# Identity products as fillers in TensorE's waits at the seam between forward and backward

## The chip, the cores and the metric

One core of a Trainium2 chip. The metric is the device time of one execution in microseconds. The kernel before has a median of 1434.71 us over three runs.

## What is computed

A decode step of an adaptively modulated transformer block and its gradients, in bfloat16: one query token, 32 heads of 192 with a cache of 8192 keys and values each, then a small MLP. The kernel returns the block's output and the gradients of nine inputs, the whole K and V caches among them.

```python
mod = (silu(c) @ w_mod).reshape(6, ...)            # sa, ca, ga, sb, cb, gb
h  = layernorm(x) * (1 + ca) + sa
q  = (h @ wq)                                      # 32 heads x 192
p  = softmax(q @ k_cache.T * 192 ** -0.5)          # 8192 positions a head
x  = x + ga * ((p @ v_cache) @ wo)
h  = layernorm(x) * (1 + cb) + sb
x  = x + gb * (h + gelu(layernorm(h) @ w3) @ w4)   # the mixing part has one position: it adds nothing
# returned: x and the gradients of x, k_cache, v_cache, wq, wo, w3, w4, c, w_mod
```

With one query, dV of a head is the outer product of its softmax weights and the gradient of its output, dK that of its score gradients and the query. The score gradients need V times the output gradient over all positions.

## The kernel before

**Forward.** A loop over heads streams K and V in halves of 4096 positions (tiles KB and VB, 128 partitions x 32 positions x 192). It ends with the MLP and its backward.

**The seam.** After the last head come the MLP's matmuls, the layer-norm gradients lb2 and lb1, `do_mm` (output gradient of a pair of heads, broadcast over partitions, tile do_r) and `c_ps` (one correction per head). Nearly all of it is one chain of small operations. `layernorm_bwd` builds lb_pr on VectorE, gets two means from a TensorE matmul into PSUM (`mean_mm`, tile mean_ps), calls `fill()` if it has one, and then reads the means (lb_s, line 128). In lb2 the fill transposes the second half of a block of wo (`do_t(TL, 8)`).

**Backward.** 64 steps (32 heads x 2 halves, from the last head down). A step s

- reduces dP out of PSUM (line 314) and forms dS on VectorE,
- makes dV in eight groups (`dv_groups`): four TensorE matmuls of one row each into a two-bank PSUM tile (line 877; two such tiles exist), then one ScalarE evacuation (line 878),
- multiplies V of the next step with do_r on VectorE in two halves (`mul_q`, line 857) and sums each product on TensorE with 12 matmuls of 128x256 against the identity (`tree_q`, line 866, here called a tree),
- makes dK in two halves on VectorE (`dk_part`, line 882),
- stores dV and dK through POOL's queue, and loads V of step s+4 through SP's (line 295).

Output tiles rotate through five buffers, V through three. A prologue ahead of step 0 makes the first half of dV and the products for step 0. Steps 0 and 1 (the last head) also get their query gradient from the K tile (`dq_rows`: dq_ps, then two pairs of matmuls into columns 0 and 1 of dq_c at lines 1109 and 1110, read on VectorE at lines 1111 and 1112).

**Side work.** Four times in a step, `slot()` runs the next piece of a list: w4 and w3 gradients, transposes of wo (wT_ps, line 746), broadcasts (bc_t, bc_ps), later the gradients of wq and w_mod.

**Order.** The program order is the order of each engine; it is written out by hand (`manual_schedule` over TensorE, VectorE, ScalarE and SyncE). Waits between engines come from the tiles' uses. All small PSUM results share one buffer, tag "s" of pool psS, one bank.

Of the kernel before, what the change touches and what calls it, by code (L numbers as in the profile page):

```python
# [8 lines left out]
FP32 = mybir.dt.float32  # L9
# [11 lines left out]
def kernel(  # L21
# [27 lines left out]
    P = 128  # L49
    D = A_x.shape[-1]  # L50
    _, HQ, S, DH = A_k_cache.shape
# [9 lines left out]
    ND = D // P  # L61
# [56 lines left out]
        return tmp.tile([P, n], dtype, name=name)  # L118


    def mean_mm(src, n):
        ps = psS.tile([P, 16], FP32, name="mean_ps", tag="s")
        T_.matmul(ps[:, 0:n], lhsT=onesD, rhs=src, start=True, stop=True)
        return ps

# [38 lines left out]
    def layernorm_bwd(dn, n, r, add, out, name, fill=None):  # L164
        pr = tcol(2 * ND, "lb_pr")
        V_.tensor_copy(out=pr[:, 0:ND], in_=dn)
        V_.tensor_tensor(out=pr[:, ND : 2 * ND], in0=dn, in1=n, op=ALU.mult)
        s = mean_cols(pr, 2, "lb_s", fill)
        t1 = tcol(ND, "lb_t1")
        V_.tensor_scalar(out=t1, in0=n, scalar1=s[:, 1:2], scalar2=s[:, 0:1], op0=ALU.mult, op1=ALU.add)  # L170
        t2 = tcol(ND, "lb_t2")
        V_.tensor_tensor(out=t2, in0=dn, in1=t1, op=ALU.subtract)
        V_.scalar_tensor_tensor(out=out, in0=t2, scalar=r[:, 0:1], in1=add, op0=ALU.mult, op1=ALU.add)

    def bcast_cols(src, n, out, eng):
        tp = psS.tile([NF, P], FP32, name="bc_t", tag="s")
        T_.transpose(out=tp[0:n, :], in_=src, identity=ident_f)
        rows = tmp.tile([NF, P], BF16, name="bc_rows")
        eng(out=rows[0:n, :], in_=tp[0:n, :])
        for g in range(0, n, 4):  # L180
            m = min(4, n - g)
            ps = psB.tile([P, 512], FP32, name="bc_ps", tag="b")
            for b in range(m):
                T_.matmul(ps[:, b * P : (b + 1) * P], lhsT=pick(n, g + b), rhs=rows[0:n, :], start=True, stop=True)
            eng(out=out[:, g * P : (g + m) * P], in_=ps[:, 0 : m * P])

    def store_vec(src, dram, name):
        tp = psS.tile([NF, P], FP32, name="sv_t", tag="s")
        T_.transpose(out=tp[0:ND, :], in_=src, identity=ident_f)
        rows = tmp.tile([ND, P], BF16, name="sv_rows")  # L190
        V_.tensor_copy(out=rows, in_=tp[0:ND, :])
        nc.gpsimd.dma_start(out=dram.rearrange("o (i p) -> (o i) p", p=P), in_=rows)
# [581 lines left out]
    n2_bf = tcol(ND, "n2_bf", BF16)  # L774
    V_.tensor_copy(out=n2_bf, in_=n2)
    w3t(2)()
    ups = psS.tile([P, NF], FP32, name="u_ps", tag="s")
    for a in range(NF):
        for k in range(ND):
            T_.matmul(ups[:, a : a + 1], lhsT=w3v[k][:, a * P : (a + 1) * P], rhs=n2_bf[:, k : k + 1], start=(k == 0), stop=(k == ND - 1))  # L780
# [30 lines left out]
                T_.matmul(h2_ps[:, k : k + 1], lhsT=w4r(a)[:, k * P : (k + 1) * P], rhs=g_bf[:, a : a + 1], start=(a == 0), stop=(a == NF - 1))  # L811

    h2_mm(0, 2)
    dn_ps = psS.tile([P, ND], FP32, name="dn_ps", tag="s")
    for k in range(ND):
        for a in range(NF):
            T_.matmul(dn_ps[:, k : k + 1], lhsT=w3Tv[a][:, k * P : (k + 1) * P], rhs=du_bf[:, a : a + 1], start=(a == 0), stop=(a == NF - 1))
# [12 lines left out]
    V_.tensor_copy(out=d_n2, in_=dn_ps)  # L830
    h2_mm(2, ND)
    do_t(TL, 0)
    layernorm_bwd(d_n2, n2, r2, dbo, d_sb, "lb2", lambda: do_t(TL, 8))
    d_n1 = tcol(ND, "d_n1")
    V_.scalar_tensor_tensor(out=d_n1, in0=cb, scalar=1.0, in1=d_sb, op0=ALU.add, op1=ALU.mult)
    dw4_rows(flat(KX), 0, 3)
    dw4_store(flat(KX), 0, 3)
    V_.tensor_tensor(out=bo, in0=h2_ps[:, 0:ND], in1=h_b, op=ALU.add)
    layernorm_bwd(d_n1, n1, r1, dy_c, dx1, "lb1")
    V_.tensor_tensor(out=dao_bf, in0=dx1, in1=ga, op=ALU.mult)  # L840
    do_mm(TL)
    V_.tensor_tensor(out=dao, in0=dx1, in1=ga, op=ALU.mult)
    V_.tensor_tensor(out=ao, in0=aoP, in1=aoN, op=ALU.add)

    c_ps = psS.tile([P, HQ], FP32, name="c_ps", tag="s")
    for k in range(ND):
        T_.matmul(c_ps, lhsT=dao[:, k : k + 1].to_broadcast([P, P]), rhs=AO[:, k, :], start=(k == 0), stop=(k == ND - 1))
    V_.tensor_tensor(out=cpr, in0=c_ps, in1=rinv, op=ALU.mult)
# [16 lines left out]
        for k in range(0, DH, TS):  # L865
            T_.matmul(ps[:, q * JQ : (q + 1) * JQ, :], lhsT=ident_bf, rhs=pq[:, q, :, k : k + TS], start=(k == 0), stop=(k == DH - TS), skip_group_check=True)  # L866

    def dv_groups(dV, er, doh, gs):

        dV4 = dV.rearrange("p (r k) d -> p r (k d)", r=4)  # L870
        for g in gs:
            m, q = divmod(g, 2)
            ps = psV.tile([P, 2, 512], FP32, name="dv_ps", tag="v")
            for k in range(2):
                for b in range(2):
                    p0 = 32 * (2 * q + b)
                    T_.matmul(ps[:, b, k * DH : (k + 1) * DH], lhsT=er[p0 : p0 + 1, 2 * m + k, :], rhs=doh[p0 : p0 + 1, :], start=True, stop=True)  # L877
            A_.copy(out=dV4[:, 2 * q : 2 * q + 2, m * PW : (m + 1) * PW], in_=ps[:, :, 0:PW])  # L878

    def dk_part(dK, qh, dS4, lo, hi):  # L880
        n = hi - lo
# [25 lines left out]
            cur["next"] = w  # L907

    def g_bcast(src, n, out):
        tp = psS.tile([NF, P], FP32, name="bc_t", tag="s")  # L910
        T_.transpose(out=tp[0:n, :], in_=src, identity=ident_f)
        rows = tmp.tile([NF, P], BF16, name="bc_rows")
        V_.tensor_copy(out=rows[0:n, :], in_=tp[0:n, :])
        yield
        for g in range(0, n, 4):
            m = min(4, n - g)
            ps = psB.tile([P, 512], FP32, name="bc_ps", tag="b")
            for b in range(m):
                T_.matmul(ps[:, b * P : (b + 1) * P], lhsT=pick(n, g + b), rhs=rows[0:n, :], start=True, stop=True)
            A_.copy(out=out[:, g * P : (g + m) * P], in_=ps[:, 0 : m * P])  # L920
            yield
# [15 lines left out]
    def g_chunk(b, first, v3, rows, dst, n, acc, lay):  # L937

        lo = n * CW
        if first:  # L940
            cur["w"] = cur.pop("next")
        w = stg = cur["w"][:, :, b * PW : (b + 1) * PW]
        cols = lambda a, b_: [(l, r, w[:, a, c0 : c0 + r - l]) for bb, l, r, c0 in lay if bb == b_]
        v_bf = tcol(3, "v_bf", BF16)
        V_.tensor_copy(out=v_bf, in_=v3)
        yield
        wT = bst.tile([P, 15 * P], BF16, name="wT", tag="wT")
        transposed(0, cols, ND, wT)
        tp = psS.tile([NF, P], FP32, name="bc_t", tag="s")
        T_.transpose(out=tp[0:3, :], in_=v3, identity=ident_f)  # L950
        vrow = tmp.tile([3, P], BF16, name="vrow")
        V_.tensor_copy(out=vrow, in_=tp[0:3, :])
        yield
        transposed(8, cols, ND, wT)
        bp = psB.tile([P, 512], FP32, name="bc_ps", tag="b")
        for bb, l, r, c0 in lay:
            T_.matmul(bp[:, c0 : c0 + r - l], lhsT=pick(3, bb), rhs=vrow[:, l:r], start=True, stop=True)
        v_bc = bst.tile([P, PW], BF16, name="v_bc")
        A_.copy(out=v_bc, in_=bp[:, 0:PW])  # L959
        yield  # L960
        ps = psS.tile([P, ND], FP32, name="acc_ps", tag="s")
        for i in range(ND):
            for bb in range(3):
                T_.matmul(ps[:, i : i + 1], lhsT=wT[:, (bb * ND + i) * P : (bb * ND + i + 1) * P], rhs=v_bf[:, bb : bb + 1], start=(bb == 0), stop=(bb == 2))
        for i in range(3):
            V_.tensor_scalar(out=stg[:, i, :], in0=v_bc, scalar1=rows[:, i : i + 1], scalar2=None, op0=ALU.mult)
        yield
        V_.tensor_tensor(out=acc, in0=ps, in1=acc, op=ALU.add)
        for i in range(3, ND):
            V_.tensor_scalar(out=stg[:, i, :], in0=v_bc, scalar1=rows[:, i : i + 1], scalar2=None, op0=ALU.mult)  # L970
        if first:
            next_w()
        else:
            nc.gpsimd.dma_start(out=dst[:, :, lo : lo + CW], in_=cur["w"])
        yield
# [124 lines left out]
    def dq_rows(t, kb, dS4):  # L1100

        ps = psB.tile([P, 512], FP32, name="dq_ps", tag="b")
        for j in range(JH):
            p0 = 32 * (j % 4)
            T_.matmul(ps[p0 : p0 + 32, 0:DH], lhsT=dS4[:, j, 0:1].to_broadcast([P, 32]), rhs=kb[:, j, :], start=(j < 4), stop=(j >= JH - 4), skip_group_check=True)
        row = bst.tile([P, DH], FP32, name="dq_junk")
        A_.copy(out=row, in_=ps[:, 0:DH])
        cp = psS.tile([P, 4], FP32, name="dq_c", tag="s")
        T_.matmul(cp[:, 0:1], lhsT=row[:, 0:P], rhs=c32[:, 0:1], start=True, stop=True)
        T_.matmul(cp[64:128, 1:2], lhsT=row[:, P:DH], rhs=c32[:, 0:1], start=True, stop=True)  # L1110
        V_.tensor_tensor(out=dq_x[:, 2:3], in0=cp[:, 0:1], in1=dq_x[:, 2:3], op=ALU.add)
        V_.tensor_tensor(out=dq_x[64:128, 1:2], in0=cp[64:128, 1:2], in1=dq_x[64:128, 1:2], op=ALU.add)
# [5 lines left out]
    dV0 = OB[0]  # L1118
    er = er_l.pop(0)
    ps = psR.tile([P, JH, TS], FP32, name="dot_ps")  # L1120
    dv_groups(dV0, er, do_of(H1), (0, 2))
    mul_q(0, 0)
    tree_q(ps, 0)
    dv_groups(dV0, er, do_of(H1), (4, 6))
    dv_store(0, dV0, 0, JQ)
    mul_q(0, 1)
    tree_q(ps, 1)
    for s in range(NS):
        h, t = ht(s)
        nxt = s + 1 < NS  # L1130
        doh = do_of(h)
        qh = qs_bc[:, h * DH : (h + 1) * DH]
        assert not nxt or (s + 1) // 4 in done
        dP = tcol(JH, "dP")
# [10 lines left out]
        slot()  # L1145
        dV, dK = OB[(2 * s) % len(OB)], OB[(2 * s + 1) % len(OB)]
        if s == 0:
            dv_groups(dV, er, doh, (1, 3))
        else:
            er = er_l.pop(s)  # L1150
            dv_groups(dV, er, doh, (0, 1, 2, 3))
        if nxt:
            ps = psR.tile([P, JH, TS], FP32, name="dot_ps")
            mul_q(s + 1, 0)
# [1 line left out]
        slot()  # L1156
        dk_part(dK, qh, dS4, 0, JQ)
        if s > 0:
            dv_groups(dV, er, doh, (4, 5))
        slot()  # L1160
        dv_groups(dV, er, doh, (5, 7) if s == 0 else (6, 7))
        if s + 2 < NS:
            er_l[s + 2] = load_er(s + 2)
        dv_store(s, dV, JQ if s == 0 else 0, JH)
# [45 lines left out]
```

## Time and profile before

| what | value |
|---|---|
| runs | 1433.92, 1434.71, 1446.62 us |
| profiled execution, its own time | 1435.39 us |
| its span, first to last instruction | 1433.6 us |
| mean granted TensorE clock | 0.766 |
| busy, PE / DVE / ACT | 78% / 77% / 61% |
| moved by DMA | 569.37 MB, 397 GB/s over the span |
| TensorE matmuls | 12739 |

The span is cut into 40 slices of 35.8 us. The clock rows give what was granted in tenths of full speed. A row of the table of stretches gives the length, the busy time of each engine with its instructions in brackets, the granted clock, the DMA engines' busy share and GB/s. In the timeline and the chain, a row starts with its start and its length in us; brackets at the end give the engine's idle time before it and what ended that.

### The profile page before, as it was taken

Reading aid. Unit: us, or ns where it says so; the run is one execution under the profiler, and the core shown is the slowest. Engines: PE = TensorE matmul, PEld = TensorE weight load, DVE = VectorE, ACT = ScalarE, POOL = GpSimd, SP = SyncE. Lnnn points to the kernel's source line nnn. Section 1 sums busy time; section 2 is a strip of 40 time slices with the busy share of each in tenths; the row PEclk is TensorE's granted clock in tenths of the full one; section 3 lists DMA queues with packets and bytes.
Section 4 is the critical chain, followed back from the end, with each engine's and each line's share of the span. In section 5 each row is a group of like instructions: output and inputs, shape, how many; then the busy total and the mean of one; then the engine's idle time right before and its main releaser. Section 6 shows DMA issues by size and latency. Waiting matters only on the chain.

```text
span 1433.6 us, 30378 instructions
## 1 busy us (share of the span) xinstructions
PE 1112.0 (78%) x12739; PEld 788.9 (55%) x12739; DVE 1100.2 (77%) x1397; ACT 880.0 (61%) x1965; POOL 144.9 (10%) x255
## 2 busy tenths in 40 slices
PE   3988989999999998775687776777767577777764
PEld 2777777777877777543444443444434344444432
DVE  4989899999999987456677676667767667676764
ACT  0777777777877776554665565556655556555644
POOL 0000000000000000111111111111111111111111
PEclk9999999999999998565656566566666766656565
DMA  9999999999999994489999999999999999999997
GB/s 375 397 418 418 411 417 415 414 416 413 418 415 411 420 411 180 156 308 407 423 406 425 423 417 423 409 419 417 418 426 427 403 425 418 422 414 416 416 406 315
DMA packets 77432, 569.37 MB, mean 397 GB/s; under 512 B 8782, under 2 KB 26526, under 8 KB 36974
## 3 DMA queue, kind: packets, MB, share of 16 engines
q1 hardware_dynamic: 50842, 340.44, 58.8%
q0 software_dynamic: 26432, 226.97, 37.7%
q8 instruction: 100, 1.64, 0.5%
q14 instruction: 38, 0.31, 0.1%
q10 hardware_dynamic: 20, 0.00, 0.0%
HBM read 340.95 MB, written 226.43 MB: 396 GB/s over the span
## 4 chain that ended last, share of the span: by engine, by line
PE 24%; DMA 11%; DVE 10%; issue 8%; ACT 7%; POOL 1%; POOLq 0%; ACTq 0%; SPq 0%; DVEq 0%
PE dot_ps L866 15%; DVE pq L857 5%; ACT KB L878 5%; DMA out_dram<-KB 4%; DMA er_b<-eT_d 4%; PE wT_ps L746 3%; PE dv_ps L877 3%; DMA VB<-in_A_v_cache_dram 2%; ACT wT L747 1%; DVE KB L882 1%; DMA wo_st<-in_A_wo_dram 1%; DVE dP L314 1%; PE do_ps L759 1%; DVE dq_junk L986 1%; ACT v_bc L959 0%
## 5 line engine op out<-in xcount | busy, mean ns | idle before, releaser
L878 ACT CAST KB<-dv_ps 128x768 bf16<-128x768 f32 x512 | 375.9, 815 | 170.5 <-PE dv_ps L877 170.2
L866 PE MATMUL dot_ps<-pq,ident_bf 128*128 128x256 bf16 x1536 | 325.7, 395 | 51.0 <-DVE pq L857 50.7
L357 ACT ACTIVATE vs<-VB,Ef 128x192 bf16<-128x192 bf16 x872 | 315.0, 447 | 0.0
L877 PE MATMUL dv_ps<-do_r,er_b 1*128 1x192 bf16 x2048 | 174.3, 311 | 147.2 <-ACT KB L878 132.6
L866 PEld LDWEIGHTS <-ident_bf 128*128 128x128 bf16 x1536 | 201.9, 135 | 152.0 <-issue 79.1
L882 DVE TENSOR_TENSOR KB<-qs_bc,dS 128x3072 bf16<-128x3072 bf16 x128 | 223.9, 1750 | 26.0 <-DMA out_dram<-KB 19.6
L300 DVE TENSOR_TENSOR prod<-KB,qs_bc 128x6144 bf16<-128x6144 bf16 x62 | 207.8, 3352 | 29.1 <-DMA KB<-in_A_k_cache_dram 17.5
L857 DVE TENSOR_TENSOR pq<-VB,do_r 128x3072 bf16<-128x3072 bf16 x126 | 220.3, 1749 | 2.7 <-DMA VB<-in_A_v_cache_dram 2.7
L877 PEld LDWEIGHTS <-er_b 1*128 1x128 bf16 x2048 | 64.8, 102 | 243.9 <-issue 225.7
L372 PE MATMUL mp<-vs,KB 128*128 128x193 bf16 x1984 | 189.8, 248 | 4.0 <-ACT vs L357 2.9
L372 PEld LDWEIGHTS <-KB 128*128 128x128 bf16 x1984 | 169.9, 98 | 13.2 <-DMA KB<-in_A_k_cache_dram 5.9
L747 ACT COPY wT<-wT_ps 128x1024 bf16<-128x1024 bf16 x84 | 81.0, 964 | 156.6 <-PE wT_ps L746 156.6
L310 PE MATMUL half_ps<-prod,ident_bf 128*128 128x256 bf16 x744 | 95.1, 279 | 46.0 <-DVE prod L304 45.7
L350 DVE TENSOR_TENSOR vs<-VB,E 128x1728 bf16<-128x1728 bf16 (+1 forms) x122 | 127.1, 1062 | 0.3 <-ACT vs L357 0.3
L314 DVE TENSOR_REDUCE dP<-dot_ps 128x32 f32<-128x512 f32 x64 | 44.1, 688 | 97.8 <-PE dot_ps L866 97.7
L304 DVE TENSOR_TENSOR prod<-prod 128x3072 bf16<-128x3072 bf16 x62 | 108.7, 1753 | 1.0
L310 PEld LDWEIGHTS <-ident_bf 128*128 128x128 bf16 x744 | 72.9, 99 | 64.2 <-issue 55.2
L377 PE MATMUL mp<-vs,KB 128*64 128x193 bf16 x1984 | 106.5, 250 | 0.0
L377 PEld LDWEIGHTS <-KB 128*64 128x64 bf16 x1984 | 79.6, 110 | 19.6 <-issue 19.6
L337 ACT ACTIVATE E<-S_h,negm 128x256 bf16<-128x256 f32 x31 | 15.8, 508 | 115.6 <-DVE negm L498 113.3
L704 POOL DMA_DIRECT2D er_b<-eT_d x64 | 36.9, 577 | 488.4 <-PE dv_ps L877 474.5
L432 POOL DMA_DIRECT2D eT_d<-er x16 | 8.8, 548 | 555.2 <-ACT vs L348 517.7
(269 smaller groups left out, 1008.0 us busy)
## 6 DMA issues: line engine op xcount, KB each, us to landing
out_dram<-KB POOLq DMA_DIRECT2D x127, 1536.0 KB, 17.1
VB<-in_A_v_cache_dram SPq DMA_DIRECT2D x123, 1536.0 KB, 12.0
KB<-in_A_k_cache_dram SPq DMA_DIRECT2D x64, 1536.0 KB, 11.3
wo_st<-in_A_wo_dram SPq DMA_DIRECT2D x31, 480.0 KB, 11.8
w_st<-in_A_wq_dram SPq DMA_DIRECT2D x12, 960.0 KB, 12.9
out_dram<-wo_st POOLq DMA_DIRECT2D x16, 480.0 KB, 18.9
out_dram<-stg POOLq DMA_DIRECT2D x7, 960.0 KB, 18.7
out_dram<-w_st POOLq DMA_DIRECT2D x7, 960.0 KB, 21.8
```

The lines of the kernel that those rows point to most:

```text
L300: V_.tensor_tensor(out=prod, in0=src, in1=vec[:, None, :].to_broadcast([P, JH, DH]), op=ALU.mult)
L304: V_.tensor_tensor(out=prod[:, :, 0:HW], in0=prod[:, :, 0:HW], in1=prod[:, :, DH - HW : DH], op=ALU.add)
L310: T_.matmul(ps, lhsT=ident_bf, rhs=prod[:, :, k : k + TF], start=(k == 0), stop=(k == w - TF))
L350: V_.tensor_tensor(out=vs[:, 0:n, 0:DH].rearrange("p j (a b) -> p j a b", b=4), in0=v[:, v0 : v0 + n, :].rearrange("p j (a b) -> p j a b", ...
L357: A_.activation(out=vs[:, k, 0:DH], in_=v[:, v0 + k, :], func=ACT.Copy, scale=Ef[:, j0 + k : j0 + k + 1])
L372: T_.matmul(mp[:, 0:MW], lhsT=kb[:, j0 + k, 0:P], rhs=vs[:, k, 0:MW], start=(q == 0 and k == 0), stop=(z and k == JQ - 1), skip_group_chec ...
L377: T_.matmul(mp[p0 : p0 + 64, MO : MO + MW], lhsT=kb[:, j0 + k, P:DH], rhs=vs[:, k, 0:MW], start=False, stop=(z and k >= JQ - 2), skip_grou ...
L857: V_.tensor_tensor(out=pq[:, q], in0=v_l[s][:, q * JQ : (q + 1) * JQ, :], in1=do_of(ht(s)[0])[:, None, :].to_broadcast([P, JQ, DH]), op=AL ...
L866: T_.matmul(ps[:, q * JQ : (q + 1) * JQ, :], lhsT=ident_bf, rhs=pq[:, q, :, k : k + TS], start=(k == 0), stop=(k == DH - TS), skip_group_c ...
L877: T_.matmul(ps[:, b, k * DH : (k + 1) * DH], lhsT=er[p0 : p0 + 1, 2 * m + k, :], rhs=doh[p0 : p0 + 1, :], start=True, stop=True)
L878: A_.copy(out=dV4[:, 2 * q : 2 * q + 2, m * PW : (m + 1) * PW], in_=ps[:, :, 0:PW])
L882: V_.tensor_tensor(out=dK[:, lo:hi, :].rearrange("p j (a b) -> p j a b", b=4), in0=qh.rearrange("p (a b) -> p a b", b=4)[:, None, :, :].to ...
```

## The change

Every tile of tag "s" that is made in these parts now comes from `s_tile`, as the front of a whole bank of 512 columns, and `s_bank` remembers the latest. `keep(n)` issues n matmuls of 128x256, the identity against a part of qs_bc, into columns 256 to 511 of that latest bank. Nothing reads these columns. `keep` is called in the two layer-norm gradients, in the prologue, and behind each dV group of steps 0 to 5. The five other tiles that now come from `s_tile` (bc_t twice, sv_t, u_ps, acc_ps) are changed in the same one-line manner.

```diff
+    s_bank = {}
+    def s_tile(n, name, rows=P):
+        s_bank["t"] = psS.tile([P, 512], FP32, name=name, tag="s")
+        return s_bank["t"][0:rows, 0:n]
+    def keep(n):
+        for _ in range(n):
+            T_.matmul(s_bank["t"][:, 256:512], lhsT=ident_bf, rhs=qs_bc[:, 0:256], start=True, stop=True, skip_group_check=True)
+
     def mean_mm(src, n):
-        ps = psS.tile([P, 16], FP32, name="mean_ps", tag="s")
+        ps = s_tile(16, "mean_ps")
...
-    dn_ps = psS.tile([P, ND], FP32, name="dn_ps", tag="s")
+    dn_ps = s_tile(ND, "dn_ps")
...
-    layernorm_bwd(d_n2, n2, r2, dbo, d_sb, "lb2", lambda: do_t(TL, 8))
+    layernorm_bwd(d_n2, n2, r2, dbo, d_sb, "lb2", lambda: (do_t(TL, 8), keep(4)))
...
-    layernorm_bwd(d_n1, n1, r1, dy_c, dx1, "lb1")
+    layernorm_bwd(d_n1, n1, r1, dy_c, dx1, "lb1", lambda: keep(6))
...
-    c_ps = psS.tile([P, HQ], FP32, name="c_ps", tag="s")
+    c_ps = s_tile(HQ, "c_ps")
...
-    def dv_groups(dV, er, doh, gs):
+    def dv_groups(dV, er, doh, gs, busy=0):
...
             A_.copy(out=dV4[:, 2 * q : 2 * q + 2, m * PW : (m + 1) * PW], in_=ps[:, :, 0:PW])
+            keep(busy)
...
-        cp = psS.tile([P, 4], FP32, name="dq_c", tag="s")
+        cp = s_tile(4, "dq_c")
...
-    dv_groups(dV0, er, do_of(H1), (0, 2))
+    dv_groups(dV0, er, do_of(H1), (0, 2), 3)
...
-    dv_groups(dV0, er, do_of(H1), (4, 6))
+    dv_groups(dV0, er, do_of(H1), (4, 6), 1)
...
+        busy = 2 if s < 6 else 0
...
-            dv_groups(dV, er, doh, (1, 3))
+            dv_groups(dV, er, doh, (1, 3), busy)
...
-            dv_groups(dV, er, doh, (0, 1, 2, 3))
+            dv_groups(dV, er, doh, (0, 1, 2, 3), busy)
...
-            dv_groups(dV, er, doh, (4, 5))
+            dv_groups(dV, er, doh, (4, 5), busy)
...
-        dv_groups(dV, er, doh, (5, 7) if s == 0 else (6, 7))
+        dv_groups(dV, er, doh, (5, 7) if s == 0 else (6, 7), busy)
```

More of the change, by code (lines that the diff above doesn't have):

```diff
@@ L175, in bcast_cols @@
     def bcast_cols(src, n, out, eng):
-        tp = psS.tile([NF, P], FP32, name="bc_t", tag="s")
+        tp = s_tile(P, "bc_t", NF)
         T_.transpose(out=tp[0:n, :], in_=src, identity=ident_f)
@@ L187, in store_vec @@
     def store_vec(src, dram, name):
-        tp = psS.tile([NF, P], FP32, name="sv_t", tag="s")
+        tp = s_tile(P, "sv_t", NF)
         T_.transpose(out=tp[0:ND, :], in_=src, identity=ident_f)
@@ L776 @@
     w3t(2)()
-    ups = psS.tile([P, NF], FP32, name="u_ps", tag="s")
+    ups = s_tile(NF, "u_ps")
     for a in range(NF):
@@ L909, in g_bcast @@
     def g_bcast(src, n, out):
-        tp = psS.tile([NF, P], FP32, name="bc_t", tag="s")
+        tp = s_tile(P, "bc_t", NF)
         T_.transpose(out=tp[0:n, :], in_=src, identity=ident_f)
@@ L948, in g_chunk @@
         transposed(0, cols, ND, wT)
-        tp = psS.tile([NF, P], FP32, name="bc_t", tag="s")
+        tp = s_tile(P, "bc_t", NF)
         T_.transpose(out=tp[0:3, :], in_=v3, identity=ident_f)
@@ L960, in g_chunk @@
         yield
-        ps = psS.tile([P, ND], FP32, name="acc_ps", tag="s")
+        ps = s_tile(ND, "acc_ps")
         for i in range(ND):
```

## The prediction

> **What bounds the kernel now.** I read the granted clock of the core first (mean 0.766), then the 40 slices of the page.
>
> ```profile
> PEclk9999999999999998565656566566666766656565
> DMA  9999999999999994489999999999999999999997
> ```
>
> In the forward pass TensorE has its full clock, in the backward about six tenths of it. The DMA engines are busy nearly everywhere but in slices 16 to 18. The table of stretches says it more sharply (length, then busy us of PE, PEld, DVE, ACT and POOL, granted clock, DMA share, GB/s):
>
> ```profile
> 585.00:640.00 55.00, 40.37 (x313) 24.59 (x312) 33.13 (x33) 31.55 (x47) 7.77 (x13) 0.56 0.68 245
> 640.00:1380.00 740.00, 534.33 (x4442) 321.91 (x4440) 523.84 (x764) 419.31 (x589) 119.96 (x205) 0.63 1.01 418
> ```
>
> From 640 us on the kernel is bound by bytes: 418 GB/s, the rate that the forward has too. A faster TensorE buys nothing there. Only the seam between the passes can give time back. From 585 to 640 us 245 GB/s move instead of 418, which is 55 x (1 - 245/418) = 22.8 us of missing transfers. Until about 592 us there is hardly anything to move: the first dV store is issued at 591.77 us. So some 7 us of this can't be filled and about 15 us is the most that faster steps can win. That is hardly more than 1% of the time (14.3 us), which is about what a measurement of this kernel can tell from no change.
>
> In the chain of work that ended last, restricted to 584 to 640 us, the trees of line 866 hold 35.5%, more than anything else. One of them here, and one late in the backward at the full clock (timeline):
>
> ```profile
> 586.73 2.72 PE dot_ps L866 x12
> 688.60 1.48 PE L866 MATMUL dot_ps<-pq,ident_bf 128*128 128x256 bf16 x12
> ```
>
> So the clock is worth 1.24 us a tree. A single slow one of these matmuls takes 0.421 us and a fast one 0.269; the spacing is therefore (2.72 - 0.42)/11 = 0.21 us slow and (1.48 - 0.27)/11 = 0.11 us fast. A filler has the same form, 128x256 against the identity, and costs the same.
>
> **When the clock rises.** The clock changes in steps of 3.41 us, so I cut the seam into stretches of that length, along its changes:
>
> ```profile
> 584.30:587.72 3.42, 1.85 (x14) 1.23 (x14) 3.08 (x6) 1.50 (x2) 0.00 (x0) 0.50 0.20 72
> 587.72:591.13 3.41, 3.41 (x22) 2.05 (x20) 0.62 (x1) 1.16 (x2) 0.00 (x0) 0.50 0.00 0
> ...
> 597.96:601.37 3.41, 3.41 (x22) 2.06 (x21) 1.03 (x1) 2.76 (x4) 1.83 (x3) 0.50 0.45 98
> ...
> 611.61:615.02 3.41, 3.41 (x21) 1.69 (x19) 0.00 (x0) 0.19 (x1) 0.00 (x0) 0.50 0.42 177
> 615.02:618.44 3.42, 2.07 (x27) 1.39 (x20) 1.94 (x2) 3.33 (x6) 0.58 (x1) 1.00 0.10 18
> ...
> 632.09:635.50 3.41, 3.15 (x18) 2.11 (x17) 2.27 (x3) 0.97 (x2) 1.65 (x3) 0.50 0.69 202
> 635.50:638.92 3.42, 1.18 (x23) 0.67 (x20) 3.38 (x4) 2.74 (x5) 0.00 (x0) 1.00 1.02 304
> ```
>
> A stretch is granted the full clock for what the one before it did. Busy time is not the measure: 587.72 and 597.96 are filled without a gap, and the clock stays at half. They hold almost one tree each, cut at an edge, and dV matmuls of a single row. The stretch from 611.61 has 8 tree matmuls and five do_ps of 384 columns, together 15.5 fillers' worth; that from 632.09 has a whole tree and four broadcasts. So some 12 full matmuls of 256 columns (3072 columns) in one stretch are the threshold, and several stretches lie just under it.
>
> The Trainium skill, "TensorE: Matmul & The Clock Gate", section "What's actually happening", puts the window at 3413 ns and grants the full clock after one busy window. The length agrees with the 3.41 us here; if any busy matmul counted, 587.72 would already have raised the clock, and it didn't.
>
> **The change, part by part.** By the diff I count 4 + 6 fillers in the two layer-norm gradients, 3 x 2 + 1 x 2 in the prologue, 2 x 4 in step 0 and 2 x 8 in each of steps 1 to 5: 106, a little below the 110 of its title. No transfer is added or moved; bank "s" keeps its one buffer.
>
> *Layer-norm gradients.* The fillers go into the bank that holds the means, between the mean matmul and its reader lb_s. Does the reader wait for them, though it reads other columns? The dq_c tile answers:
>
> ```profile
> 603.70 0.59 PE L1109 MATMUL dq_c<-c,dq_junk 128*128 128x1 f32 x2 [0.43 <-ACT dq_junk L1107]
> 604.22 0.37 PE L1110 MATMUL dq_c<-c,dq_junk 128*64 128x1 f32 x2
> 604.63 0.16 DVE L1111 TENSOR_TENSOR dq_x<-dq_c,dq_x 128x1 f32<-128x1 f32 x1 [5.64 <-PE dq_c L1110]
> ```
>
> Line 1111 reads column 0, which line 1109 wrote, and still it starts only behind line 1110, which writes column 1. So I take it that a reader waits for every earlier write into its tile. The Trainium skill, "PSUM — Partial Sum Buffer", section "PSUM bank collisions raise a hardware error", asks for the same: guard by bank, not by address. This speaks against an "unread part" being free; by addresses alone this term would be 0.85 us.
>
> The stage before the change:
>
> ```profile
> 577.25 0.17 DVE L128 TENSOR_REDUCE lb_s<-mean_ps 128x2 f32<-128x10 f32 x1 [1.74 <-PE mean_ps L123]
> 577.98 0.91 PE L746 MATMUL wT_ps<-ident_bf,wo_st 128*128 128x128 bf16 x7 [0.76 <-ACT wT L747]
> 578.82 0.57 PE L123 MATMUL mean_ps<-lb_pr,onesD 128*128 128x10 f32 x2
> 579.43 0.17 DVE L128 TENSOR_REDUCE lb_s<-mean_ps 128x2 f32<-128x10 f32 x1 [0.76 <-PE mean_ps L123]
> 580.65 0.82 PE L759 MATMUL do_ps<-wT,dao_bf 128*128 128x384 bf16 x2 [1.25 <-DVE dao_bf L840]
> ```
>
> The first lb_s now waits for the transposes (end 578.89) and 4 x 0.21: 579.75 instead of 577.25, 2.5 us later. From there to the second mean matmul it is 1.42 us of VectorE (lb_pr ends at 578.67), then 0.58, then 6 x 0.21 = 1.28: the second lb_s starts at 583.05 instead of 579.43. do_ps starts 3.65 us later. The clock is half here, and the 7 x 128 + 4 x 256 = 1920 columns ahead of it don't raise it. Taken: **+3.65**, since the dq_x row is the nearest; lower bound +0.85, where only TensorE's order delays the second mean.
>
> *Fillers in the prologue and the steps.* The six behind groups 0 and 2 take 1.28 us and lie in TensorE's wait of 1.57 us for the first pq product; without that cover they would cost their 1.28. In a step, a group's matmuls wait for ScalarE's evacuation (0.60 us each: 132.6 us over 220 waits), which covers 2 fillers at 0.42. Uncovered are those of the last group before a tree: 0.42 us at half clock in the prologue, 0.84 a step. Only steps 0 to 2 come ahead of saturation: 0.42 + 3 x 0.84 = 2.9 slow, 1.5 fast. Taken: **+2.2**. Bounds: nothing, if all are covered, and 106 x 0.21 = 22.3 us together with the layer norms, if none is.
>
> *The clock.* On the chain seven trees between 586 and 636 us run slow: 7 x 1.24 = 8.7 us. Its other TensorE pieces there (dV groups, dq, transposes, do_ps) sum to 8.8 us; of these I give 3.5 to the clock, less than half, as latency doesn't shrink. Always fast would be worth 12.2 us. How much of it comes? Of the 14 half-clock stretches from 584.30 to 635.50, the tree matmuls number 5, 14, 9, 11, 14, 3, 0, 6, 8, 5, 0, 9, 5 and 12. Sixteen fillers over a step of 11 to 17 us are about 4 a stretch. With these, 7 of 14 pass twelve (counting do_ps). So I take half: **-6.1**, between 0 and 12.2.
>
> Sum: 3.65 + 2.2 - 6.1 = -0.25 us. The profiled execution has a span of 1433.6 and a time of 1435.39; the runs have a median of 1434.71. On the median that gives **1434.5 us**.
>
> **Rivals.**
> *The clock holds.* Once fast, a step is shorter, its columns are denser, and no stretch falls below the threshold until step 6. For it: several stretches lie just under twelve. Against: TensorE still waits for ScalarE (2.9 us for four evacuations), where two fillers per 0.7 us are only 10 a stretch. Time: 3.65 + 1.5 - 12.2 = -7 us, 1427.7; with the reader not waiting, 1424.9. This is also what the skill's rule of any busy window would make of it.
> *The fillers only queue: slower.* The clock stays at half from do_ps on; TensorE, in order, does its fillers ahead of the next tree, and the first stores come later. It decides from the point where clearly fewer than half of the stretches rise, for at half the sum is nought; with none it is 3.65 + 2.9 = +6.5 us, **1441.2**; with the covers gone too, up to 1457. For it: the fillers' first ten lie in a stage with few columns. Against: 587.72 needs two or three more.
> *The lead is lost in the transfers.* From 618 us the DMA share is 0.9 or more, so only the five trees before it count: half of 5 x 1.24 = 3.1 is won, 3.65 + 2.2 paid, +2.8 us, 1437.5. Against: holes of 0.44 to 0.69 up to 635 us.
>
> **How the numbers follow.** Forecast 0.45, clock holds 0.25, fillers queue 0.2, lost in transfers 0.1. The range runs from 1424 (clock holds, no wait for lb_s) to 1446 (queueing, with two thirds of the further covers kept). Faster by over 1% would need the whole 15 us of fillable transfers, 0.12; slower by over 1% would need some two thirds of all fillers uncovered, 0.14; the rest, 0.74, is within 1%.
>
> **What would show it.** Right: the second lb_s some 3.6 us later, beginning behind a filler; full clock in about half of the stretches from 588 to 640 us; the dP reduce of step 4 (now at 648.73) within 4 us of that; 418 GB/s unchanged behind it. Wrong: an lb_s ahead of the fillers; a clock that stays full from 588 us on, or at half; DMA saturated more than 5 us earlier or later than 640.

## The result, and the profile after

The changed kernel has a median of 1442.24 us over 20 runs (1435.31 to 1447.59), the kernel before, on the same chip, 1435.93 us over 20 (1431.05 to 1446.62). The ratio is 1.0042 with a 95% interval of 1.0027 to 1.0057: about 6.0 us slower. That is inside the range and, as forecast, within 1%, but the forecast was no change, and the kernel became slower by more than its interval.

The page of the profile after shows the clock and the DMA engines' share in 40 slices of 36.0 us:

```profile
span 1440.0 us, 30591 instructions
PEclk7899999999999998667556566556665666656656
DMA  9999999999999994389999999999999999999998
```

The low stretch of the DMA row lies in the same slices as before and is a little deeper (4, 3, 8 instead of 4, 4, 8). The table of stretches for the same two windows as before (length, busy us of PE, PEld, DVE, ACT and POOL, clock, DMA share, GB/s):

```profile
585.00:640.00 55.00, 47.41 (x358) 25.98 (x359) 30.49 (x41) 29.28 (x43) 7.78 (x13) 0.69 0.62 227
640.00:1380.00 740.00, 544.00 (x4476) 325.98 (x4475) 522.26 (x763) 419.94 (x590) 118.20 (x202) 0.64 1.01 415
```

So the clock did rise in the seam, from 0.56 to 0.69, and yet fewer bytes move there: 227 GB/s instead of 245.

The layer-norm gradients in the timeline after:

```profile
578.42 0.55 PE L135 MATMUL mean_ps<-lb_pr,onesD 128*128 128x10 f32 x2
580.42 1.06 PE L131 MATMUL mean_ps<-qs_bc,ident_bf 128*128 128x256 bf16 x4
581.52 0.17 DVE L140 TENSOR_REDUCE lb_s<-mean_ps 128x2 f32<-128x10 f32 x1 [4.26 <-PE mean_ps L131]
583.52 1.44 PE L131 MATMUL mean_ps<-qs_bc,ident_bf 128*128 128x256 bf16 x6
585.00 0.17 DVE L140 TENSOR_REDUCE lb_s<-mean_ps 128x2 f32<-128x10 f32 x1 [2.05 <-PE mean_ps L131]
586.21 1.78 PE L771 MATMUL do_ps<-wT,dao_bf 128*128 128x384 bf16 x5 [1.26 <-DVE dao_bf L852]
```

Line 131 is the filler in `keep`, line 140 the read of the means. The first mean is complete at 578.97, but lb_s starts at 581.52, 0.04 us behind the last filler, and its idle time is put down to line 131. The second lb_s does the same.

The forward of this execution came 1.75 us later, so times below are counted from the copy of d_n out of PSUM ahead of the first layer-norm gradient (575.08 us before, 576.83 us after). A second profile of the changed kernel (the last experiment) agrees with the first to 0.3 us in every column.

| from the d_n copy, us | do_ps | dP step 0 | step 2 | step 4 | step 5 | step 6 | full clock up to 72 us, start (length) |
|---|---|---|---|---|---|---|---|
| before | 5.57 | 17.8 | 49.1 | 73.7 | 86.3 | 103.5 | 39.9 (3.4), 60.4 (3.4), 67.3 (3.4) |
| after | 9.39 | 22.3 | 50.3 | 77.5 | 90.9 | 109.5 | 22.8 (10.2), 39.9 (10.2), 70.6 (3.4) |

By these two profiles the changed kernel is 4.5 us late at step 0, wins 3.3 of it back in steps 0 and 1, where it has full clock for part of the time, and loses 2.6 again in steps 2 and 3 at half clock. At step 6 it is 6.0 us late. The loss in steps 2 and 3 comes again in the second profile (27.3 us for the two, 24.6 before); whether the 3.3 us are owed to the fillers is taken up at e9_late_only.

### The profile page after: what moved, and what is told of

Its sections match the earlier page's. It is cut to its first block, busy times and chain, and to the rows that moved or that the text cites. A ratio compares the mean times of both kernels' runs of the same rounds, so it can differ in the third digit from the quotient of the medians.

```text
span 1440.0 us, 30591 instructions
## 1 busy us (share of the span) xinstructions
PE 1133.2 (79%) x12845; PEld 796.4 (55%) x12845; DVE 1101.1 (76%) x1397; ACT 881.1 (61%) x1965; POOL 144.8 (10%) x255
## 4 chain that ended last, share of the span: by engine, by line
PE 26%; DVE 10%; issue 8%; ACT 8%; DMA 7%; POOL 1%; POOLq 0%; ACTq 0%; DVEq 0%
PE dot_ps L878 16%; DVE pq L869 5%; ACT KB L890 5%; PE wT_ps L758 3%; PE dv_ps L889 3%; DMA er_b<-eT_d 3%; DMA VB<-in_A_v_cache_dram 2%; DMA out_dram<-KB 1%; ACT wT L759 1%; DVE KB L895 1%; DVE dP L326 1%; PE do_ps L771 1%; DMA out_dram<-stg 1%; DVE dq_junk L999 1%; ACT v_bc L972 1%
## 5 line engine op out<-in xcount | busy, mean ns | idle before, releaser
L878 PE MATMUL dot_ps<-pq,ident_bf 128*128 128x256 bf16 x1536 | 322.0, 392 | 50.5 <-DVE pq L869 50.1
## 6 DMA issues: line engine op xcount, KB each, us to landing
VB<-in_A_v_cache_dram SPq DMA_DIRECT2D x123, 1536.0 KB, 11.6
```

## The experiments

Ratios are against the kernel before on the same chip, with 95% intervals; a thousandth is 1.4 us. Diffs are against the changed kernel. The relative times are from one profile each. LN fillers are the ten in the layer-norm gradients, group fillers the 96 in the prologue and behind the dV groups of the steps.

| kernel | LN fillers | group fillers | ratio | us | dP step 0 | dP step 4 | clock 585 to 640 us |
|---|---|---|---|---|---|---|---|
| before | none | none | 1 | 0 | 17.8 | 73.7 | 0.56 |
| after | means' bank | 96 | 1.0042 [1.0027, 1.0057] | +6.0 | 22.3 | 77.5 | 0.69 |
| e1_ln_only | means' bank | none | 1.0029 [1.0013, 1.0045] | +4.2 | 21.6 | 77.6 | 0.56 |
| e2_no_ln | none | 96 | 1.0012 [0.9991, 1.0033] | +1.7 | 18.5 | 73.9 | 0.69 |
| e3_ln_other_bank | free bank | 96 | 0.9989 [0.9971, 1.0007] | -1.6 | 18.2 | 72.9 | 0.73 |
| e4_one_row | means' bank, one row | 96, one row | 1.0044 [1.0026, 1.0063] | +6.3 | 22.3 | 79.6 | 0.59 |
| e5_two_steps | free bank | prologue, steps 0, 1 | 0.9974 [0.9956, 0.9992] | -3.7 | 14.3 | 67.2 | 0.81 |
| e6_before_tree | free bank | the same, 4 ahead of a tree in steps 2 to 5 | 0.9957 [0.9939, 0.9974] | -6.2 | 18.2 | 71.9 | 0.71 |
| e7_one_each | free bank | 1 a group in the steps | 0.9983 [0.9967, 0.9999] | -2.4 | 17.6 | 72.5 | 0.72 |
| e8_four_each | free bank | 4 a group in the steps | 0.9984 [0.9970, 0.9997] | -2.3 | 14.3 | 68.1 | 0.88 |
| e9_late_only | none | steps 2 to 5 | 0.9999 [0.9982, 1.0015] | -0.1 | 17.1 | 70.7 | 0.69 |
| e10_denser_ln | free bank, closer | prologue, steps 0, 1 | 0.9967 [0.9947, 0.9986] | -4.7 | 13.8 | 67.0 | 0.81 |
| e11_ln_other_only | free bank | none | 0.9977 [0.9963, 0.9991] | -3.3 | 16.7 | 71.4 | 0.60 |

**Only the LN fillers (e1_ln_only).**

```diff
-    dv_groups(dV0, er, do_of(H1), (0, 2), 3)
+    dv_groups(dV0, er, do_of(H1), (0, 2))
...
-    dv_groups(dV0, er, do_of(H1), (4, 6), 1)
+    dv_groups(dV0, er, do_of(H1), (4, 6))
...
-        busy = 2 if s < 6 else 0
+        busy = 0
```

> Only the 4 + 6 fillers of the layer-norm gradients are kept. Theory (the means' readers wait for the fillers, and the seam's delay goes straight into the end): do_ps starts 9.4 us after the copy of d_n, as in the changed kernel, instead of 5.6; the clock afterwards as before the change; time +3 to +4 us (ratio 1.002 to 1.003). Rival (the later DMA-bound part takes the delay up): do_ps as late, time within 1 us of before.

Measured: +4.2 us, between 1.9 and 6.5. do_ps comes 9.38 us behind the d_n copy as in the whole change, and step 4 is 3.9 us late. The ten fillers alone cost about what do_ps is late.

**Only the group fillers (e2_no_ln).** The two layer-norm gradients are called as before.

```diff
-    layernorm_bwd(d_n2, n2, r2, dbo, d_sb, "lb2", lambda: (do_t(TL, 8), keep(4)))
+    layernorm_bwd(d_n2, n2, r2, dbo, d_sb, "lb2", lambda: do_t(TL, 8))
...
-    layernorm_bwd(d_n1, n1, r1, dy_c, dx1, "lb1", lambda: keep(6))
+    layernorm_bwd(d_n1, n1, r1, dy_c, dx1, "lb1")
```

> Only the fillers behind the dV groups are kept, none in the layer-norm gradients. Theory: 3.8 us better than the whole change, so +1 to +3 us against before (1.001 to 1.002): the groups still run at 0.97 us each at half clock. Rival (the step fillers are harmless and the layer norms are the whole loss): 0 us or faster. Second rival (the layer norms' fillers are what first raises the clock): the clock stays at half up to step 1 and the time is no better than with the whole change.

Measured: +1.7 us, between -1.3 and +4.7. do_ps is back at 5.57, the clock is as high as in the whole change, and step 4 comes 0.2 us later than before. So 96 fillers with all the clock they bring win nothing that can be measured here; the 3.9 us of gain that the prediction's terms add up to (+2.2 - 6.1) lie outside the interval. The two parts, +4.2 and +1.7, add up to the whole.

**The LN fillers in another bank (e3_ln_other_bank).** The same ten matmuls write a dV tile that nobody uses at that time.

```diff
+    v_bank = psV.tile([P, 2, 512], FP32, name="dv_ps", tag="v")
+    def keep_v(n):
+        for _ in range(n):
+            T_.matmul(v_bank[:, 0, 0:256], lhsT=ident_bf, rhs=qs_bc[:, 0:256], start=True, stop=True, skip_group_check=True)
...
-    layernorm_bwd(d_n2, n2, r2, dbo, d_sb, "lb2", lambda: (do_t(TL, 8), keep(4)))
+    layernorm_bwd(d_n2, n2, r2, dbo, d_sb, "lb2", lambda: (do_t(TL, 8), keep_v(4)))
...
-    layernorm_bwd(d_n1, n1, r1, dy_c, dx1, "lb1", lambda: keep(6))
+    layernorm_bwd(d_n1, n1, r1, dy_c, dx1, "lb1", lambda: keep_v(6))
```

> The whole change, but the 4 + 6 fillers of the layer-norm gradients write into a free dV tile, which nothing reads before the prologue. Theory: both lb_s start ahead of the fillers; do_ps only 0.9 us later than before the change; time 3 us better than the whole change, about +2 to +3 us (1.0015 to 1.002). Rival (the delay is TensorE's order, not the bank): as late as with the whole change, 1.004.

Its timeline, around the second layer norm:

```profile
575.75 0.55 PE L135 MATMUL mean_ps<-lb_pr,onesD 128*128 128x10 f32 x2
576.34 0.17 DVE L140 TENSOR_REDUCE lb_s<-mean_ps 128x2 f32<-128x10 f32 x1 [1.74 <-PE mean_ps L135]
577.76 1.06 PE L849 MATMUL dv_ps<-qs_bc,ident_bf 128*128 128x256 bf16 x4
578.61 0.44 PE L135 MATMUL mean_ps<-lb_pr,onesD 128*128 128x10 f32 x2
578.90 1.44 PE L849 MATMUL dv_ps<-qs_bc,ident_bf 128*128 128x256 bf16 x6
579.09 0.17 DVE L140 TENSOR_REDUCE lb_s<-mean_ps 128x2 f32<-128x10 f32 x1 [1.33 <-PE mean_ps L135]
580.30 1.78 PE L771 MATMUL do_ps<-wT,dao_bf 128*128 128x384 bf16 x5
```

Both lb_s now start 0.04 us behind the mean matmul (line 135), the second in the middle of the six fillers (line 849). The second mean still queues behind the four fillers, so do_ps is 0.57 us later than before instead of 3.82. The ratio falls from 1.0042 to 0.9989: 7.6 us (4.2 to 11.0, with both intervals), with nothing changed but the tile into which ten results go. The other tile lies in another bank too, so no run here tells whether it is the tile or the bank that sets the wait.

**All fillers one row high (e4_one_row).** As many matmuls of as many columns at the same places, but with one partition of the array.

```diff
-            T_.matmul(s_bank["t"][:, 256:512], lhsT=ident_bf, rhs=qs_bc[:, 0:256], start=True, stop=True, skip_group_check=True)
+            T_.matmul(s_bank["t"][:, 256:512], lhsT=ident_bf[0:1, :], rhs=qs_bc[0:1, 0:256], start=True, stop=True, skip_group_check=True)
```

> All 106 fillers as in the change, but each uses one row of the identity and one row of the moving data, as the dV matmuls do: the same time on TensorE, hardly any activity in the array. Theory (the clock follows array columns, and fillers in a slow queue cost time): the clock stays at half through the prologue and steps 0 and 1, groups take about 0.9 us, the trees 2.7; +8 to +13 us (1.006 to 1.009). Rival (any busy matmul raises the clock): clock and time as with the whole change, +6 us.

Measured: +6.3 us; the two spells of 10.2 us of full clock in steps 0 and 1 are gone (full only at 33.3, 43.5 and 50.4 us for 3.4 us each). do_ps is at 9.58. Against the changed kernel that is 0.3 us, with some 3.4 us of uncertainty on either side: the clock that the fillers bring is worth between -3.1 and 3.7 us in the time, not 6.1. The time is near its rival's +6 us; the clock (0.59) is nearer to the theory's. One caveat: these fillers overlap with the one-row dV matmuls, which full ones don't, so they cost a little less in TensorE's queue (the two groups behind the first tree of the prologue take 1.17 us with their fillers instead of 1.38).

**Group fillers in the prologue and two steps only (e5_two_steps).** The edit of e3_ln_other_bank, and:

```diff
-        busy = 2 if s < 6 else 0
+        busy = 2 if s < 2 else 0
```

> The change with the layer-norm fillers in the free dV tile, and fillers behind the dV groups only in the prologue and steps 0 and 1. Theory (the fillers win 2 to 3 us while the clock is full in steps 0 and 1, and lose it again in steps 2 to 5, where at half clock a group with its two fillers takes 0.97 us instead of ScalarE's 0.70): dP of step 2 comes 3 us earlier after the copy of d_n than before the change, and stays so to step 6; time -2 to -3 us (0.998). Rival (what is won in the first steps is lost in the transfers in any case): dP of step 2 as early, but the time within 1 us of before.

Measured: -3.7 us. The profile has full clock from 6.0 to 26.5 us and is 6.5 us ahead at step 4. Leaving out the fillers of steps 2 to 5 gave 0.15% against e3_ln_other_bank, with overlapping intervals.

**Fillers ahead of a tree instead (e6_before_tree).** The edit of e5_two_steps, and four fillers into the PSUM half that the first tree of steps 2 to 5 then overwrites:

```diff
-    def tree_q(ps, q):
+    def tree_q(ps, q, pre=0):
+        for _ in range(pre):
+            T_.matmul(ps[:, q * JQ : (q + 1) * JQ, :], lhsT=ident_bf, rhs=qs_bc[:, 0:256].rearrange("p (a b) -> p a b", b=TS), start=True, stop=True, skip_group_check=True)
...
+        pre = 4 if 2 <= s < 6 else 0
...
-            tree_q(ps, 0)
+            tree_q(ps, 0, pre)
```

> As the kernel with fillers in steps 0 and 1 alone, and in steps 2 to 5 four fillers ahead of the first tree, where TensorE waits for VectorE's product, instead of two behind each dV group. Theory: groups stay at 0.70 us, trees of these steps partly at full clock; steps 2 to 5 no slower than before the change; time -2 to -4 us (0.998). Rival (any filler in these steps delays the chain): no better than with two fillers behind each group and the free dV tile, 0.999 to 1.001.

Measured: -6.2 us, the fastest of all. But its profile has no full clock in steps 2 to 5, and these steps are no shorter (dP of step 2 to step 4: 25.7 us, e5_two_steps 24.4). Why it should beat e5_two_steps isn't seen, the two intervals overlap, and the plain medians of the two are alike, 1434.70 and 1434.53 us.

**One or four fillers a group (e7_one_each, e8_four_each).** The edit of e3_ln_other_bank, and:

```diff
-        busy = 2 if s < 6 else 0
+        busy = 1 if s < 6 else 0
```

```diff
-        busy = 2 if s < 6 else 0
+        busy = 4 if s < 6 else 0
```

> The change with the layer-norm fillers in the free dV tile, and one filler instead of two behind each group of steps 0 to 5. Theory: a group with one filler takes 0.70 to 0.75 us at half clock, so steps 3 to 5 lose nothing; but fewer columns, so the full clock holds for fewer stretches in steps 0 and 1: dP of step 2 some 1.5 us earlier than before the change; time -1 to -2 us. Rival (the clock is all that matters): less full clock, worse than with two.

> The change with the layer-norm fillers in the free dV tile, and four fillers instead of two behind each group of steps 0 to 5. It measures what a clock that stays full to step 5 is worth. If the clock holds (about 15 fillers' worth a stretch) a group takes 0.75 to 0.85 us; theory (behind a full clock VectorE's four products of 1.67 us and ScalarE's evacuations are the next bound): a step of 11.5 us as step 0 has with the change, and a time of -2 to +1 us. Rival of the prediction (a held clock is worth 7 to 12 us): -7 us or better, 0.995.

Measured: -2.4 and -2.3 us, with two fillers -1.6: the number hardly matters. With four, the clock is full for most of the first steps; the table of stretches of e8_four_each:

```profile
585.00:600.00 15.00, 12.66 (x114) 8.54 (x115) 9.88 (x13) 11.89 (x19) 2.76 (x4) 1.00 0.32 119
600.00:660.00 60.00, 53.27 (x470) 31.56 (x468) 37.37 (x49) 32.12 (x47) 10.46 (x18) 0.83 0.88 338
```

It is the kernel with the most clock. It is 5.6 us ahead at step 4 and 2.3 in the time; the rival's 7 us of gain lie outside its interval (0.4 to 4.3).

**Fillers in steps 2 to 5 only (e9_late_only).** No LN fillers, none in the prologue.

```diff
-        busy = 2 if s < 6 else 0
+        busy = 2 if 2 <= s < 6 else 0
```

> Fillers behind the dV groups of steps 2 to 5 alone, none in the layer norms, the prologue and steps 0 and 1. Theory A (these fillers are what turns the step fillers from a gain into a loss, since DMA isn't yet saturated there): steps 2 to 5 take 2 to 3.5 us longer than before the change, and the time is +1.5 to +3 us (1.001 to 1.002). Theory B (the transfers take it up): steps 2 to 5 longer, but the time within 1 us of before (0.9993 to 1.0007).

Measured: 0.9999, between -2.6 and +2.2 us, so the lower end of theory A isn't excluded. In its profile dP goes from step 2 to step 5 in 38.8 us, 37.2 before. Its longer steps aren't found in the time.

This profile shows one thing more. Up to step 2 the program is that of the kernel before, and yet it takes 28.1 us for steps 0 and 1, where the profile before has 31.3 (e1_ln_only and e11_ln_other_only, without a filler there either, 31.1 and 29.9). It has full clock from 16.2 and from 23.0 us, which the profile before hasn't. So the 28.0 us of the changed kernel can't be put down to its fillers, and a lead in the table above can be 4 us of chance; only the ratios average over it.

**LN fillers closer together (e10_denser_ln).** The edit of e5_two_steps, but:

```diff
-    layernorm_bwd(d_n2, n2, r2, dbo, d_sb, "lb2", lambda: (do_t(TL, 8), keep(4)))
+    layernorm_bwd(d_n2, n2, r2, dbo, d_sb, "lb2", lambda: (keep_v(3), do_t(TL, 8), keep_v(1)))
```

> As the kernel with fillers in steps 0 and 1 alone, but the layer-norm fillers (in the free dV tile) stand as 3 ahead of the second half of the transposes, where TensorE waits for ScalarE, 1 behind them and 6 behind the second mean. Theory (a full clock from do_ps on is worth 3.5 us at dP of step 0, and comes when the columns ahead of do_ps lie densely in one 3.41 us stretch): do_ps at most 0.4 us later than before, full clock by 9 us after the copy of d_n, time -3 to -6 us (0.996 to 0.998). Rival (where the stretches fall decides, not four fillers): as with two steps, 0.9974, give or take its interval.

Measured: -4.7 us, do_ps at 5.57 as before, full clock from 5.8 us, and 6.7 us ahead at step 4. Against e5_two_steps the gain isn't beyond the intervals.

**The LN fillers alone, in the other bank (e11_ln_other_only).** The edits of e1_ln_only and e3_ln_other_bank together.

```diff
-    layernorm_bwd(d_n1, n1, r1, dy_c, dx1, "lb1", lambda: keep(6))
+    layernorm_bwd(d_n1, n1, r1, dy_c, dx1, "lb1", lambda: keep_v(6))
...
-        busy = 2 if s < 6 else 0
+        busy = 0
```

> Only the 4 + 6 fillers of the layer-norm gradients, in the free dV tile; none behind dV groups. Against the kernel with the same ten in the means' bank (+4.2 us) this shows the bank alone. Theory: do_ps 0.6 us later than before; time 0 to -2 us, so 3 to 6 us better than in the means' bank. Rival (ten fillers cost by TensorE's order): +2 us or more.

Measured: -3.3 us, against +4.2 in the means' bank: 7.5 us apart (4.4 to 10.6, with both intervals), as with the group fillers (7.6). The timeline has the do_ps matmuls at full clock:

```profile
582.85 0.99 PE L771 MATMUL do_ps<-wT,dao_bf 128*128 128x384 bf16 x5
```

At half clock they take 1.78 us. So ten of the fillers, put elsewhere, give as much, within the intervals, as the versions with 62, 106 or 194.

**The changed kernel again (after_again).** No edit.

> The changed kernel once more, for its profile. Theory (the stretches of the clock don't start with the kernel): other stretches between the copy of d_n and step 5 have the full clock than in the first profile, and dP of step 0 moves by up to 4 us with them; lb_s and do_ps at the same distance from the copy of d_n, 8.2 and 9.4 us. Rival (the stretches follow the kernel): the same stretches, dP of step 0 22.3 us after the copy of d_n.

Measured: full clock at 23.1 and 40.2 us, for 10.2 us each, where the first profile has 22.8 and 39.9; dP of step 0 is at 22.3 in both. The low clock in the prologue of the changed kernel belongs to the kernel; that it was a matter of chance in the first profile is refuted as far as a second profile can.

## Why the prediction was wrong, by its steps

**Bound by bytes from 640 us on, seam only: right for the place, wrong for the exchange.** The transfers stay at 415 GB/s, and the changed kernel's 6.0 us at step 6 are 4.6 at the end (863.1 us from the d_n copy, 858.5 before). But a lead was counted in full, and it isn't. e8_four_each, e5_two_steps and e10_denser_ln are 5.6, 6.5 and 6.7 us ahead at step 4, and gain 2.3, 3.7 and 4.7 us in the timed runs; their profiled executions take 857.7, 857.6 and 856.4 us from the d_n copy to the end, which keeps 0.8, 0.9 and 2.1 us of the lead. The chain that ended last shows one place where a lead goes: TensorE waits for a block of wo. First the kernel before, then e10_denser_ln:

```profile
659.04 15.32 DMA wo_st<-in_A_wo_dram
```

```profile
653.72 17.43 DMA wo_st<-in_A_wo_dram
```

Counted from the d_n copy, the load starts 6.5 us earlier and arrives 4.4 us earlier: 2.1 us of the lead are spent in this one transfer, while the DMA engines are full in both (share 1.01 and 1.00, 426 and 415 GB/s). That the rest of it is lost in the same way later on wasn't shown piece by piece.

**Layer-norm gradients, +3.65: right.** do_ps is 3.82 us later, by the mechanism forecast, a reader that waits for writes into columns it doesn't read. The Trainium skill, "PSUM — Partial Sum Buffer", section "PSUM bank collisions raise a hardware error", asks to guard by bank; the rows of lb_s after agree, with 2.5 us of wait for the first. The term was right in size and too narrow in what hangs on it: moving the ten results is worth 7.5 us, of which 3.24 are do_ps (9.38 to 6.14 in the pair without group fillers). What is left lies behind do_ps, and the clock has a part in it: in the versions with the free bank the first full stretch starts at 5.8 to 8.6 us (e7_one_each: 15.9), in the changed kernel at 22.8. Counted as in the last section, six of these seven have a stretch of 3139 to 3430 columns between the d_n copy and the end of do_ps (e7_one_each: 2973), for there the ten fillers fall into one stretch with the transposes or with do_ps. In the changed kernel and e1_ln_only, where the reader waits, the fillers are spread out and no stretch there has more than 2172. How much of the rest this explains isn't shown; the sum had no term for it.

**Fillers in the prologue and the steps, +2.2: the size in the time right, the cover wrong.** The prologue cost 0.7 us (do_ps to dP of step 0: 12.9 us against 12.2), 0.42 forecast. In the steps, two fillers were to fit under the 0.60 us for which a group waits for ScalarE. The timeline of the changed kernel at half clock:

```profile
632.55 0.50 PE L889 MATMUL dv_ps<-do_r,er_b 1*128 1x192 bf16 x4
632.98 0.61 PE L131 MATMUL dq_c<-qs_bc,ident_bf 128*128 128x256 bf16 x2
633.52 0.50 PE L889 MATMUL dv_ps<-do_r,er_b 1*128 1x192 bf16 x4
633.96 0.61 PE L131 MATMUL dq_c<-qs_bc,ident_bf 128*128 128x256 bf16 x2
634.06 0.80 ACT L890 CAST KB<-dv_ps 128x768 bf16<-128x768 f32 x1 [0.17 <-PE dv_ps L889]
```

From one group to the next it is 0.97 us: 0.43 of dV matmuls and 0.54 of two fillers, not 0.42. ScalarE, which takes 0.70 us from one evacuation to the next when it isn't held up (1.50 us for two), now waits for TensorE. The cover has turned round. This makes steps 2 and 3 of the changed kernel 2.6 us longer than before, where the sum had 0.84 for step 2 and nothing for step 3. How much of it reaches the end isn't resolved: e9_late_only costs nothing measurable, give or take 2.4 us.

**The clock, -6.1: this is the step that failed.** "Always fast would be worth 12.2 us" holds roughly, up to step 4 and by single profiles: e5_two_steps has 0.81 instead of 0.56 between 585 and 640 us, which is 0.57 of the way to full clock or 6.9 us by that figure, and is 6.5 us ahead. "So I take half" doesn't: in the time, the fillers behind the groups with their clock cost 1.7 us (-1.3 to 4.7, e2_no_ln), where this term and the one before promised a gain of 3.9, and taking most of their clock away changes the time by 0.3 us (e4_one_row). Six of the 16 stretches from 586 to 640.6 us are full, and the clock makes 0.30 of the way. The stretches after, five of them:

```profile
585.99:589.40 3.41, 3.19 (x14) 2.51 (x14) 0.31 (x3) 0.73 (x2) 0.00 (x0) 0.50 0.21 75
589.40:592.81 3.41, 3.41 (x20) 1.80 (x21) 2.60 (x6) 1.60 (x2) 0.00 (x0) 0.50 0.00 0
...
599.64:603.05 3.41, 2.01 (x19) 1.24 (x18) 3.38 (x4) 3.41 (x5) 0.63 (x1) 1.00 0.62 231
...
630.35:633.77 3.42, 3.42 (x21) 1.65 (x19) 2.05 (x3) 0.68 (x1) 0.55 (x1) 0.50 1.01 431
633.77:637.18 3.41, 3.26 (x20) 0.99 (x17) 2.14 (x3) 2.46 (x4) 0.48 (x1) 0.50 0.84 353
```

The threshold of 12 matmuls wasn't the mistake; the last section finds it in all profiles. The count of what a stretch would hold was. It took matmuls cut at an edge as whole (587.72 and 597.96 stand there with 14 each; by their time they hold 12.0, just too few), and it added the fillers to what was there. In a stretch that is filled already they push other matmuls out: at 0.21 us each it has room for 16, and every dV group takes 0.43 us of it with matmuls one row high. So the prologue (586 to 599.6) stays at half, although TensorE is busy nearly throughout: its first three stretches hold 2172, 2207 and 2824 columns, under 3072. There the clock is worth most: the prologue, from do_ps to dP of step 0, takes 12.9 us in the changed kernel and 8.2 in e5_two_steps, with the same fillers in it (12.1 in e3_ln_other_bank, where most of it is at half). Steps 0 and 1 are 3.3 us shorter than in the one profile before, as they are without fillers in e9_late_only. Steps 2 and 3 stay at half, because two fillers in 0.97 us are 7 a stretch, not the 10 that I counted with 0.7 us. And where the clock is full, the next bound is near:

```profile
601.93 1.49 PE L878 MATMUL dot_ps<-pq,ident_bf 128*128 128x256 bf16 x12 [1.40 <-DVE pq L869]
605.26 1.47 PE L878 MATMUL dot_ps<-pq,ident_bf 128*128 128x256 bf16 x12 [0.66 <-DVE pq L869]
```

Both trees wait for VectorE's product. Step 0 took 11.6 us instead of 13.9, 2.3 less, where two trees at 1.24 us alone were to give 2.5, and their neighbours another 1.0. Of these 3.3 us 0.7 are left at step 4 (4.5 us late at step 0, 3.8 there), and nothing beyond the intervals in the time.

**The rivals.** "The fillers only queue" had the sign and the size (+6.5 forecast, +6.0 measured). Its condition, clearly fewer than half of the stretches, was met too, but not its reason: the clock did rise in six stretches, and steps 2 and 3 became longer. That its number came out so closely is luck: it charged 3.65 + 2.9 for late matmuls and nothing for the clock, while the runs give +4.2 and +1.7 with the clock in it. "The clock holds" came true in e8_four_each only, and even there gave 2.3 us with a free bank. "The lead is lost in the transfers" is half right, as the wo load shows.

**What would have shown it.** lb_s behind a filler: yes. Half of the stretches full: no, six of 16. dP of step 4 within 4 us of 648.73: it is at 654.33, 5.6 us later, of which 1.75 came out of the forward.

**A version that beats both.** Six have an interval wholly below 1. The four lowest are e6_before_tree (0.9957), e10_denser_ln (0.9967), e5_two_steps (0.9974) and e11_ln_other_only (0.9977). Which of them is best is open, since their intervals overlap. All six have the LN fillers in the free bank.

## What to carry to other kernels

Work whose results nobody reads belongs in a tile that nobody reads, here in another bank too: the same ten matmuls cost 4.2 us in one and gained 3.3 us in the other. Count what a stretch of the clock would hold after the change at the pace that the change itself sets, and price the gain by the next engine's bound, here VectorE's products. Then ask how much of a lead the transfers behind it leave: here 5.6 to 6.7 us in the profiles became 2.3 to 4.7 us in the time.

## What the runs showed of the hardware that was not expected

**Busy isn't enough: columns of full height count.** With fillers one row high (e4_one_row), of the same number and length, TensorE is busy for 44.32 of 55 us between 585 and 640 us and the clock is 0.59; with fillers of 128 rows it is 47.41 us and 0.69. e9_late_only has 0.69 too and is less busy than either. The stretches of e4_one_row and of e9_late_only:

```profile
585.00:640.00 55.00, 44.32 (x346) 27.79 (x347) 29.16 (x40) 28.75 (x43) 7.09 (x12) 0.59 0.58 218
585.00:640.00 55.00, 43.46 (x354) 26.02 (x354) 33.49 (x37) 32.09 (x47) 7.77 (x13) 0.69 0.73 267
```

The Trainium skill, "TensorE: Matmul & The Clock Gate", section "What's actually happening", grants the full clock after one busy window of activity; by that, the one-row fillers would have done as well, and they did not.

The 14 profiles together give a sharper rule. I took the 308 stretches of 3.41 us in the first 80 us behind the d_n copy, weighted each matmul's columns by the share of the array's 128 rows and 128 columns that it uses, and spread them evenly over its time. Of 191 stretches with fewer than 3000 such columns one is followed by full clock; of 101 with 3080 or more all are; of the 16 between, nine. So the 3072 columns that the prediction read from a handful of stretches hold. Busy time tells nothing of the kind: 36 of the 75 stretches in which TensorE is busy for 3.40 us or more are followed by half clock.

**The stretches nearly follow the kernel.** The edges of the 3.41 us stretches lie between 1.67 and 2.69 us behind the d_n copy (modulo 3.41) in all 14 profiles, not spread over 3.41 us. Within this the outcome still turns: e3_ln_other_bank and e6_before_tree (1.7 and 1.8 us) reach dP of step 0 at 18.2 us, e5_two_steps and e8_four_each (2.6 and 2.5 us) at 14.3 us, with the same program up to there. Before the change it is as close: the stretch 12.6 us behind the d_n copy holds 3069 columns and is followed by half clock, the same stretch in e9_late_only (12.8 us), with the same program so far, 3088, and full clock follows. So a single profile can be 4 us off at this place, and that is why the verdicts above rest on the timed ratios.
